# Attention scores by pairs of heads on the two row halves of the TensorE array

## The chip, the cores and the metric

The kernel runs on one core of a Trainium2 chip. The metric is the device time of one execution in microseconds (us): the median of three runs was 967.11 us (966.23 to 969.17). One further execution was taken by the hardware profiler; all rows below are from it. The engines are PE (TensorE matmul), PEld (its weight loads), DVE (VectorE), ACT (ScalarE), POOL (GpSimd) and SP (SyncE, which issues the DMAs).

## The reference, cut to what matters

Attention over 4 batches, 8 heads, 576 positions and 64 channels per head, with a causal window of 128 positions, followed by two feed-forward layers over all 2304 tokens:

```python
scores = (q @ k.T) / sqrt(64)                 # per batch and head
bias   = slope[h] * -abs(i - j)               # slope[h] = 2 ** -(h + 1)
scores = where((i >= j) & (i - j < 128), scores + bias, -1e9)
attn   = exp(scores - max); attn /= attn.sum() + 1e-9
x = (attn @ v), heads side by side            # 2304 x 512
x = ((silu(x @ w_gate) * (x @ w_val)) @ w_out)    # 512 -> 1536 -> 512
y = (g(x @ w_in)) @ w_out2                    # 512 -> 2048 -> 512, g(h) = h * tanh(softplus(h))
```

Everything is float32, and the kernel keeps that precision: either with float32 matmuls, or with operands split into a rounded float32r part ("hi") and the rest ("lo"), of which several rounded matmuls are added up in PSUM.

## The kernel before, in words

**Chunks.** The tokens are cut into five chunks of 512, 384, 512, 512 and 384 (`A_CHUNKS`). A chunk is cut into blocks of up to 128 queries; where a chunk begins or ends inside a batch, a block has 64. A block with `qn` queries needs the keys of its own block and of the one before it (`kn`), so its scores are `qn` rows by `kn + qn` (128 to 256) columns of PSUM. `chunk_plan` packs a chunk's blocks into two PSUM banks of 512 columns (`p.sb`): two blocks of 256 columns and one each of 256 and 128 in chunks 0 and 2; 256+192 and 192+128 in chunk 1; 256+256 and 192+192+128 in chunk 3; 256+256 and 256 in chunk 4.

**Scores of a head.** q and k lie transposed, channels on the partitions. In the first six pairs of heads (`S_FULL`: four of chunk 0, two of chunk 1; "native") the two heads of a pair lie on partitions 0 to 63 and 64 to 127 of one float32 tile, and each head's scores are float32 matmuls over its 64 rows; the profile records two matmuls for each. In the other 14 pairs (28 heads; "split") each head is loaded by itself, twice over, into both halves of `qraw` and `kraw`; `split` makes `Q` (rows 0 to 63 rounded q, rows 64 to 127 the rest of q), `K1` (rounded k in both halves) and `KL` (the rest of k), by two ScalarE and two VectorE instructions (L193, L121, L195, L124). Then two matmuls over all 128 rows, with `K1` and `KL`, give the scores of a block. Native loads alternate between two buffers; `qraw`, `kraw`, `Q`, `K1`, `KL` have one each.

**After the scores.** Per bank VectorE copies the needed half of the window over (`copy_predicated`, L221/L228), and per block adds the bias and takes the maximum (L235); ScalarE takes the exponential with its sum (L239). Per head `norm` inverts the sums (L247, L250) and scales (ScalarE L254, in chunk 0 half on GpSimd, L256). `transp` transposes on PE (L261, into `t_ps`), ScalarE copies out (L267) and GpSimd masks into the two halves of `PT` (L270, L274). `outp` multiplies with v for a pair of heads: its matmuls alternate between column halves of the array, 64 weight columns each (`o_ps`), and the sum is split into hi and lo of `xt`.

**Order.** The first stage is the attention of chunk 0 with the conversion of the first weights beside it. Then come windows: window *ci* holds the gated layer of chunk *ci*, 24 hidden groups (`g_ps`, 12 matmuls of the chunk's columns each) and some 12 out groups (`acc`, 12 matmuls each), and between them the attention pieces of chunk *ci + 1*. The order on PE is written out by hand; the other engines and SP's DMA queue are ordered by the compiler's planner. A piece is S (the scores of one bank), T (a head's transposes) or O (`outp` of a pair), and carries a planned cost (S 1.7 native, 0.87 split; T 0.48; O 0.46 for each key block). After every group, pieces are issued as long as (groups done) x (sum of costs) / (number of groups) exceeds the cost issued so far. The pieces of a step are ordered by `CFG["order"]`: for step `st`, S and S of head `st`, O of the pair finished before, T of head `st - 1` (`st - 2` in chunk 0). With `S` of one head go at its end `norm`, the `split` of the next head and the `load` of the one after that.

**PSUM.** Scores, transposes, O and hidden groups take turns on four banks (`rot`); the four others hold the sums of the out groups.

After the windows come the last gated chunk and the second feed-forward layer (from about 523 us); the change does not touch them.

## Time and profile before

| | us |
|---|---|
| median of three runs | 967.11 |
| profiled execution | 970.98 |
| its span, first to last instruction | 968.9 |
| PE busy | 929.1 (96%) |
| PEld busy | 829.6 (86%) |
| DVE busy | 718.1 (74%) |
| ACT busy | 526.9 (54%) |
| POOL busy | 218.8 (23%) |

The span is what the profile shows; the execution takes 2.1 us more around it. Busy times of matmuls overlap, since the profile models their ends: how long a matmul holds the engine is read from one start to the next. The stages begin at 6.22 (first scores), 60.10 (window of chunk 0), 186.48 (chunk 1), 283.46 (chunk 2), 403.50 (chunk 3) and 522.52 us (last gated chunk).

### The profile page before, as it was taken

How to read it: one execution, taken by the hardware profiler on the slowest of the kernel's cores; microseconds unless marked ns; L12 is line 12 of the kernel's file. 1: busy time of each engine (PE TensorE's matmuls, PEld its weight loads, DVE VectorE, ACT ScalarE, POOL GpSimd, SP SyncE). 2: the span in 40 equal slices, each digit the busy share in tenths (PEclk: the TensorE clock that was granted, in tenths of full speed). 3: DMA queues.
4: the chain of work that ended last, by engine and by line, in shares of the span. 5: the costliest groups of instructions: out<-in, count | busy, mean ns of one | idle time of the engine just before them, and what ended most of it. 6: DMA issues, size and time to landing. Idle time of an engine off the chain costs nothing. (4 is left out here: it accounts for less than half of the span.)

```text
span 968.9 us, 14644 instructions
## 1 busy us (share of the span) xinstructions
PE 929.1 (96%) x5040; PEld 829.6 (86%) x5040; DVE 718.1 (74%) x1359; ACT 526.9 (54%) x1135; POOL 218.8 (23%) x348
## 2 busy tenths in 40 slices
PE   7789999999999999999998998899999999999998
PEld 5447777898998888887877998889999999999997
DVE  5999999788768865478534768778886788777673
ACT  6856667666666664455433445455544645454442
POOL 2531234211110322001014233552012320122000
PEclk9889999999999999999999999999999999999999
DMA  8763334476546743176306993624784257830385
GB/s 285 261 252 143 119 133 148 139 236 220 170 130 195 249 130 115 31 243 216 118 1 221 387 329 106 232 83 145 256 298 148 66 173 251 312 114 21 96 264 183
DMA packets 76921, 174.86 MB, mean 180 GB/s; under 512 B 9136, under 2 KB 52528, under 8 KB 67120
## 3 DMA queue, kind: packets, MB, share of 16 engines
q1 hardware_dynamic: 76848, 173.94, 54.1%
q8 instruction: 40, 0.66, 0.3%
q14 instruction: 33, 0.27, 0.1%
HBM read 138.25 MB, written 35.65 MB: 179 GB/s over the span
## 5 line engine op out<-in xcount | busy, mean ns | idle before, releaser
L114 PE MATMUL g_ps<-xt,w 128*128 128x512 f32 (+1 forms) x1440 | 316.3, 373 | 1.2 <-DVE xt L124 1.2
L114 PEld LDWEIGHTS g_ps<-xt,w 128*128 128x128 f32 x1440 | 258.1, 188 | 37.7 <-issue 2.0
L114 PE MATMUL bk<-xs,win 128*128 128x384 f32 x1008 | 179.0, 336 | 8.1 <-DVE G L684 6.0
L114 PEld LDWEIGHTS bk<-xs,win 128*128 128x128 f32 x1008 | 174.4, 188 | 12.2 <-DVE G L684 9.7
L114 PE MATMUL bk<-op,wout 128*128 128x384 f32 x1008 | 175.8, 334 | 0.8 <-DMA wout<-w2o 0.7
L114 PEld LDWEIGHTS bk<-op,wout 128*128 128x128 f32 x1008 | 174.8, 188 | 1.4 <-issue 1.4
L114 PE MATMUL acc<-hh,ring 128*128 128x512 f32 (+1 forms) x480 | 148.9, 373 | 1.6 <-DVE ring L124 1.5
L121 ACT ACTIVATE op<-G 128x768 fp32r<-128x768 f32 x84 | 70.7, 846 | 66.0 <-PE bk L114 63.4
L114 PEld LDWEIGHTS acc<-hh,ring 128*128 128x128 f32 x480 | 89.0, 188 | 14.9 <-DVE ring L124 2.3
L124 DVE TENSOR_TENSOR op<-G,op 128x768 fp32r<-128x768 f32 x84 | 80.2, 962 | 27.2 <-ACT op L121 26.7
L270 POOL TENSOR_SCALAR_AFFINE_SELECT PT<-PT 128x256 f32<-128x256 f32 (+4 forms) x80 | 42.6, 546 | 253.4 <-ACT PT L267 253.2
L780 POOL TENSOR_TENSOR t<-w 128x256 f32<-128x256 f32 x48 | 44.4, 945 | 224.3 <-DVE win L124 207.7
L114 PE MATMUL acc<-hl,ring 128*128 128x512 f32 (+1 forms) x240 | 88.5, 369 | 1.7 <-DVE hl L124 1.7
L239 ACT ACTIVATE Pt<-Pt,sm 128x128 f32<-128x128 f32 (+1 forms) x160 | 62.5, 392 | 21.5 <-DVE sm L235 21.2
L619 DVE SCALAR_TENSOR_TENSOR t<-t,g_ps 128x512 f32<-128x512 f32 (+1 forms) x60 | 37.6, 627 | 37.4 <-ACT t L618 37.2
L684 DVE TENSOR_TENSOR G<-u,bk 128x384 f32<-128x384 f32 x72 | 38.9, 552 | 31.3 <-PE bk L114 29.2
L1028 ACT ACTIVATE G<-G 128x384 f32<-128x384 f32 x72 | 36.9, 520 | 44.2 <-DVE G L684 44.2
L618 ACT ACTIVATE t<-g_ps 128x512 f32<-128x512 f32 (+1 forms) x60 | 32.8, 547 | 50.3 <-PE g_ps L114 50.2
L627 DVE SCALAR_TENSOR_TENSOR t<-t,g_ps 128x512 f32<-128x512 f32 (+1 forms) x60 | 37.8, 631 | 27.1 <-PE g_ps L114 26.4
L121 ACT ACTIVATE hh<-t 128x512 fp32r<-128x512 f32 (+1 forms) x60 | 35.0, 583 | 41.4 <-DVE t L627 41.4
L254 ACT ACTIVATE Pt<-Pt,sm 128x128 f32<-128x128 f32 (+1 forms) x144 | 46.3, 390 | 12.9 <-DVE sm L250 12.8
L274 POOL TENSOR_SCALAR_AFFINE_SELECT PT<-PT 128x256 f32<-128x256 f32 (+4 forms) x80 | 52.9, 678 | 1.6
(79 smaller groups left out, 1282.2 us busy)
## 6 DMA issues: line engine op xcount, KB each, us to landing
wout<-w2o SPq DMA_DIRECT2D x42, 1024.0 KB, 5.6
wraw<-w SPq DMA_DIRECT2D x16, 1024.0 KB, 5.3
w2o<-chl SPq DMA_DIRECT2D x16, 896.0 KB, 8.6
wst<-w SPq DMA_DIRECT2D x12, 1024.0 KB, 7.2
cw<-w1od SPq DMA_DIRECT2D x24, 512.0 KB, 4.0
w<-w2d SPq DMA_DIRECT2D x24, 512.0 KB, 3.4
w2d<-cw SPq DMA_DIRECT2D x16, 512.0 KB, 4.0
wraw<-w1o SPq DMA_DIRECT2D x6, 1024.0 KB, 6.4
```

The source lines that it names most:

```text
L114: nc.tensor.matmul(out=out, lhsT=lhsT, rhs=rhs, start=start, stop=stop, skip_group_check=True)
L121: return nc.scalar.activation(out=out, in_=in_, func=AF.Copy)
L124: return nc.vector.tensor_tensor(out=out, in0=in_, in1=hi.bitcast(F32), op=ALU.subtract)
L239: nc.scalar.activation(out=Pt[:q.qn], in_=Pt[:q.qn], func=AF.Exp, scale=-1.0, bias=sm[:q.qn, i:i + 1], accum_out=sm[:q.qn, 8 + i:9 + i],)
L254: nc.scalar.activation(out=pt, in_=pt, func=AF.Copy, scale=r)
L270: nc.gpsimd.affine_select(out=here, in_=prev, pattern=[[0, m], [1, n]], compare_op=ALU.is_ge, fill=0.0, base=0, channel_multiplier=-1,)
L274: nc.gpsimd.affine_select(out=prev, in_=prev, pattern=[[0, m], [-1, n]], compare_op=ALU.is_gt, fill=0.0, base=0, channel_multiplier=1,)
L619: nc.vector.scalar_tensor_tensor(out=t[:, :n], in0=t[:, :n], scalar=1.0, in1=st["g"][:, :n], op0=ALU.add, op1=ALU.mult)
L627: nc.vector.scalar_tensor_tensor(out=t[:, :n], in0=t[:, :n], scalar=0.5, in1=vps[:, :n], op0=ALU.mult, op1=ALU.mult)
L684: nc.vector.tensor_tensor(out=out, in0=a, in1=b, op=op)
L780: nc.gpsimd.tensor_tensor(out=x[:, o], in0=a, in1=b, op=ALU.subtract)
L1028: nc.scalar.activation(out=out, in_=in_, func=AF.Mish)
```

## The change

The unit of attention is now a pair of heads instead of a head.

- Loads: one tile `q` and one tile `k` per pair, the heads on partitions 0 to 63 and 64 to 127, one DMA each per segment (a chunk has one or two), for native and split pairs alike, with one buffer for each of the two. Where the chunk's last block has 64 queries, a further DMA loads 64 more columns of q.
- `split` of a split pair: `qh`, `kh` (rounded, ScalarE) and `ql`, `kl` (the rest, VectorE) over 128 partitions, once per pair.
- `score` takes two PSUM banks, one for each head, and issues for every block one pass (native: q, k) or three (split: qh kh, ql kh, qh kl); each pass is two matmuls over 64 rows, one for each head. Split passes have 128 weight columns also where the block has 64 queries.
- `norm` runs once per pair. The order of a step is S O S T T, for the scores of pair `st`, O of pair `st - 2` and the transposes of pair `st - 1`.
- The planned cost of S is worked out from its columns (0.64 to 0.72 for two blocks of a split pair, 0.53 to 0.75 for a native one) and is paid once for two heads; T and O keep theirs.

The core of the diff:

```diff
-    order="SSOT", delay0=2, early=[4], pbufs=10, pump_g=2, pump_p=2, lag=4, lastlag=6, evprio=500,
+    order="SOSTT", early=[2], pbufs=20, pump_g=2, pump_p=2, lag=4, lastlag=6, evprio=500,
...
-            elif s_full(h):
-                q = ap.tile([128, p.n], F32, tag=("qraw", "Q")[pr % 2], name="q32")
-                k = ap.tile([128, p.nk], F32, tag=("K1", "KL")[pr % 2], name="k32")
             else:
-                q = ap.tile([128, p.n], F32, tag="qraw", name="qraw")
-                k = ap.tile([128, p.nk], F32, tag="kraw", name="kraw")
+                q = ap.tile([128, nq], F32, tag="q", name="q")
+                k = ap.tile([128, p.nk], F32, tag="k", name="k")
...
+                nc.sync.dma_start(out=q[:, cq], in_=qT[s.b, hs_, :, sq].rearrange("h d s -> (h d) s"))
+                nc.sync.dma_start(out=k[:, ck], in_=kT[s.b, hs_, :, sk].rearrange("h d s -> (h d) s"))
...
+            qh = ap.tile([128, nq], F32R, tag="qh", name="qh")
+            kh = ap.tile([128, p.nk], F32R, tag="kh", name="kh")
+            nc.scalar.activation(out=qh, in_=q, func=AF.Copy, scale=c)
+            hi_act(kh, k)
+            ql = ap.tile([128, nq], F32R, tag="ql", name="ql")
+            kl = ap.tile([128, p.nk], F32R, tag="kl", name="kl")
             nc.vector.scalar_tensor_tensor(
-                out=Q[64:128], in0=q[64:128], scalar=c, in1=Q[64:128].bitcast(F32), op0=ALU.mult, op1=ALU.subtract
+                out=ql, in0=q, scalar=c, in1=qh.bitcast(F32), op0=ALU.mult, op1=ALU.subtract
             )
-            lo_dve(KL, k, K1)
-            qk[h] = (Q, K1, KL)
+            lo_dve(kl, k, kh)
+            qk[pr] = ((qh, kh), (ql, kh), (qh, kl))
...
+            s_ps = [rot("s_ps") for _ in range(2)]
...
-                    mm(o, Q[:, q.c:q.c + q.qn], K1[:, q.ko:q.ko + w], True, False)
-                    mm(o, Q[:, q.c:q.c + q.qn], KL[:, q.ko:q.ko + w], False, True)
+                m = q.qn if len(passes) == 1 else 128
+                for i, (Q, K) in enumerate(passes):
+                    for e in range(2):
+                        r = slice(64 * e, 64 * e + 64)
+                        mm(
+                            s_ps[e][:m, q.so:q.so + w], Q[r, q.c:q.c + m], K[r, q.ko:q.ko + w],
+                            i == 0, i == len(passes) - 1,
+                        )
...
-            return (a.ci, 1.7 if a.s_full(h) else 0.87, f)
+            if r < a.s_native:
+                return (a.ci, sum((q.kn + q.qn) / 600 for q in blocks), f)
+            return (a.ci, sum(3 * max((q.kn + q.qn) / 2400 + 0.013, 0.107) for q in blocks), f)
...
-            bufs = {"P": CFG["pbufs"], "sm": 8, "PT": 3}
+            bufs = {"P": CFG["pbufs"], "sm": 3, "PT": 3}
```

## Rows read from the trace of the kernel before

**Rows 1.** Stage windows: start:end, length, busy us (instructions), clock, DMA share, GB/s.

```profile
6.22:60.10 53.88, 44.15 (x160) 28.25 (x161) 44.69 (x133) 39.26 (x108) 27.98 (x40) 0.84 0.87 306
60.10:186.48 126.38, 122.58 (x614) 94.17 (x613) 119.48 (x266) 83.63 (x214) 33.69 (x57) 1.00 0.43 141
283.46:403.50 120.04, 120.04 (x642) 97.81 (x641) 80.44 (x199) 69.02 (x197) 23.24 (x70) 1.00 0.47 148
```

**Rows 2.** Waits of PE: us in total, times, longest.

```profile
PE s_ps L114 <- DVE Q L195: 4.0, 3, 1.7
```

**Rows 3.** Timeline of PE, first stage: start, us, instruction, idle before.

```profile
6.22 7.10 PE L114 MATMUL s_ps<-qkv 64*128 64x256 f32 x24 [6.22 <-ACT qkv L185]
...
29.80 1.78 PE L114 MATMUL s_ps<-qkv 64*128 64x256 f32 x8
...
33.57 3.35 PE L114 MATMUL s_ps<-qkv 64*128 64x256 f32 x8
...
42.33 0.66 PE L261 MATMUL t_ps<-cst_sb,Pt 128*128 128x128 f32 x4
...
60.10 2.81 PE L114 MATMUL g_ps<-xt,w 128*128 128x512 f32 x10
```

**Rows 4.** Window of one head's scores in the first stage, columns as above.

```profile
33.57:36.85 3.28, 3.28 (x9) 2.50 (x8) 3.28 (x14) 2.07 (x8) 3.10 (x5) 0.50 1.01 353
```

**Rows 5.** Timeline of PE around two native pieces of chunk 1.

```profile
75.46 1.16 PE L114 MATMUL s_ps<-k,q 64*128 64x256 f32 x4
76.55 0.50 PE L114 MATMUL acc<-hh,ring 128*128 128x512 f32 x1
...
79.50 0.95 PE L114 MATMUL s_ps<-k,q 64*64 64x192 f32 x4
80.38 3.96 PE L114 MATMUL g_ps<-xt,w 128*128 128x512 f32 x16
```

**Rows 6.** Timeline of PE around split pieces of chunks 1 and 4.

```profile
121.19 0.25 PE L114 MATMUL s_ps<-K,Q 128*64 128x192 f32 x1
121.28 0.25 PE L114 MATMUL s_ps<-KL,Q 128*64 128x192 f32 x1
...
418.61 0.28 PE L114 MATMUL s_ps<-K,Q 128*128 128x256 f32 x1
...
419.08 0.40 PE L114 MATMUL acc<-hh,ring 128*128 128x512 f32 x1
...
421.83 0.28 PE L114 MATMUL s_ps<-K,Q 128*128 128x256 f32 x1
```

**Rows 7.** Timeline of PE, a split piece's end and an O piece, chunk 2.

```profile
200.18 0.27 PE L114 MATMUL s_ps<-KL,Q 128*128 128x128 f32 x1
200.29 0.39 PE L114 MATMUL acc<-hh,ring 128*128 128x384 f32 x1
...
202.52 1.74 PE L114 MATMUL o_ps<-PT,v 128*64 128x256 f32 x20
204.19 2.00 PE L114 MATMUL g_ps<-xt,w 128*128 128x384 f32 x10
```

**Rows 8.** Groups by form, split on VectorE: count, busy us, mean ns, idle before.

```profile
L124 DVE TENSOR_TENSOR KL<-kraw,K 128x640 fp32r<-128x640 f32 x16 | 13.1, 820 | 0.6 <-ACT K L121 0.3
L195 DVE SCALAR_TENSOR_TENSOR Q<-qraw,Q 64x512 fp32r<-64x512 f32 x16 | 11.0, 690 | 1.4 <-ACT Q L193 0.9
```

**Rows 9.** Timeline of PE at the last O piece of attention.

```profile
508.15 0.65 PE L114 MATMUL o_ps<-PT,v 128*64 128x256 f32 x2
511.27 2.82 PE L114 MATMUL o_ps<-PT,v 128*64 128x256 f32 x14 [2.47 <-POOL PT L274]
514.02 5.95 PE L114 MATMUL g_ps<-xt,w 128*128 128x512 f32 x24
```

**Rows 10.** Timeline of SP: start, us of issuing, instruction.

```profile
44.23 2.39 SPq L167 DMA_DIRECT2D kraw<-kT  x4
```

**Rows 11.** DMA issues: count, KB each, median us from issue to landing.

```profile
kraw<-kT SPq DMA_DIRECT2D x16, 128.0 KB, 2.9
```

More of the change, by code (lines that the diff above doesn't have):

```diff
@@ L138, in attention, with load @@
         raw, qk, pt_, P_, sums = {}, {}, {}, {}, {}
-        nb_ = len(p.qb)
-        def s_full(h):
-            return h // 2 < s_native
-        def load(h):
-            pr, e = divmod(h, 2)
-            if s_full(h) and e:
-                return
+        nq = p.n + 64 * (p.qb[-1].qn == 64 and not upfront)
+        def load(pr):
             if upfront:
@@ L231, in score @@
-            for q in blocks:
-                Pt = ap.tile([128, 128], F32, tag="P", name="Pt")
-                slope = float(2.0 ** -(h + 1))
-                i = q.idx
-                nc.vector.tensor_tensor_reduce(
-                    out=Pt[:q.qn], in0=s_ps[:q.qn, q.so:q.so + 128], in1=nb[q.kn][:q.qn],
-                    op0=ALU.add, op1=ALU.min, scale=slope, scalar=3.0e38, accum_out=sm[:q.qn, i:i + 1],
-                )
-                nc.scalar.activation(
-                    out=Pt[:q.qn], in_=Pt[:q.qn], func=AF.Exp, scale=-1.0,
-                    bias=sm[:q.qn, i:i + 1], accum_out=sm[:q.qn, 8 + i:9 + i],
-                )
-                P_[h, q.idx] = Pt
@@ new lines, in score @@
+                for i, (Q, K) in enumerate(passes):
[4 more added lines that the diff above has]
+                            i == 0, i == len(passes) - 1,
+                        )
+            twin = [q for q in blocks if q.kn and q.qn == 128]
+            for e in range(2):
+                t = s_ps[e]
+                if len(twin) == 2:
+                    both = t.rearrange("p (u k c) -> p u k c", u=2, k=2)
+                    nc.vector.copy_predicated(
+                        out=both[:, :, 0], mask=own.rearrange("p (u c) -> p u c", u=2), data=both[:, :, 1]
+                    )
+                else:
+                    for q in blocks:
+                        if q.kn:
+                            a = q.so + q.kn
+                            nc.vector.copy_predicated(
+                                out=t[:q.qn, q.so:q.so + q.qn], mask=own[:q.qn, :q.qn], data=t[:q.qn, a:a + q.qn]
+                            )
+                for q in blocks:
+                    h = 2 * pr + e
+                    Pt = ap.tile([128, 128], F32, tag="P", name="Pt")
+                    i = 8 * e + q.idx
+                    nc.vector.tensor_tensor_reduce(
+                        out=Pt[:q.qn], in0=t[:q.qn, q.so:q.so + 128], in1=nb[q.kn][:q.qn],
+                        op0=ALU.add, op1=ALU.min, scale=float(2.0 ** -(h + 1)), scalar=3.0e38,
+                        accum_out=sm[:q.qn, i:i + 1],
+                    )
+                    nc.scalar.activation(
+                        out=Pt[:q.qn], in_=Pt[:q.qn], func=AF.Exp, scale=-1.0,
+                        bias=sm[:q.qn, i:i + 1], accum_out=sm[:q.qn, 16 + i:17 + i],
+                    )
+                    P_[h, q.idx] = Pt
@@ new lines, in norm @@
+        def norm(pr):
+            sm = sums.pop(pr)
+            nc.vector.tensor_scalar(out=sm[:, 16:32], in0=sm[:, 16:32], scalar1=1.0e-9, scalar2=None, op0=ALU.add)
+            nc.vector.reciprocal(out=sm[:, 32:48], in_=sm[:, 16:32])
+            for e in range(2):
+                for q in p.qb:
+                    i = 32 + 8 * e + q.idx
+                    pt, r = P_[2 * pr + e, q.idx][:q.qn], sm[:q.qn, i:i + 1]
+                    if ci or q.idx < 2:
+                        nc.scalar.activation(out=pt, in_=pt, func=AF.Copy, scale=r)
+                    else:
+                        nc.gpsimd.tensor_scalar(out=pt, in0=pt, scalar1=r, scalar2=1.0, op0=ALU.mult, op1=ALU.mult)
@@ L277, in transp @@
                 )
[L278 removed]
+            pt_[h] = pt
         def outp(pr):
```

153 lines of the change are left out of this document (51 added, 102 removed), and 3 rows, old and new, of the table full.

## The prediction, made before the changed kernel ran

> **What bounds the kernel now.** I read the stage windows first, then the waits of TensorE, then its timeline piece by piece. The windows [rows 1] divide the attention work in two. In the first stage (the attention of chunk 0, up to 60.1 us) nothing is full: PE is busy 44.15 of 53.88 us, VectorE 44.69. In the windows of the gated layer (from 60.1 us on) PE is full: 120.04 of 120.04 us in the window of chunk 2, 122.58 of 126.38 in that of chunk 0, where VectorE is nearly full too (119.48). So in the windows every nanosecond of PE issue time in a score, and every wait that PE's fixed order meets, counts one to one; in the first stage the chain from scores over VectorE, ScalarE and GpSimd back to PE counts. The largest wait of PE inside the windows that the change touches is 4.0 us for the split operand Q [rows 2].
>
> **Split scores, streaming.** The pitch is read from start to start, since the busy times of single matmuls overlap. A head now issues two matmuls per query block with all 128 rows. Two blocks of 256 columns take 419.08 - 418.61 = 0.47 us, 0.12 a matmul [rows 6]; one of 128 columns took 200.29 - 200.18 = 0.11, though its columns alone are half of that, so its 128 weight columns set it [rows 7]; one of 192 columns with 64 weight columns took 0.09 [rows 6]. So a block's two matmuls take 0.24, 0.18 and (128 columns, the first of them 0.07) 0.18 us. Per head: chunk 1 0.24 + 3 x 0.18 = 0.78 us, chunk 2 0.90, chunk 3 1.02, chunk 4 0.72; times 4, 8, 8, 8 heads that is 24.2 us, and some 1.2 us more where the weights of the next group are late after a short matmul (0.05 in half of the pieces): 25.4.
> After the change a pair needs three passes, each with the two heads on the two row halves. If the halves run side by side, a pass costs what one matmul costs now: 0.12 for 256 columns, 0.11 for shorter ones (128 weight columns everywhere now). Chunk 1: 3 x (0.12 + 3 x 0.11) = 1.35 us a pair; chunk 2: 3 x (3 x 0.12 + 0.11) = 1.41; chunk 3: 3 x (2 x 0.12 + 3 x 0.11) = 1.71; chunk 4: 9 x 0.12 = 1.08. Times 2, 4, 4, 4 pairs: 19.5 us, 5.9 less.
> Do they run side by side? The nearest row is the O piece, which alternates between column halves: 20 records, eight of 256 and twelve of 128 columns at two passes each, would take 2.99 us one after the other at 2.4 GHz and take 1.67 (204.19 - 202.52) [rows 7]. For row halves there is one hint: the first three heads' scores, laid in turn on the two halves, follow each other without a break and take 7.10 us, while one head took 3.35 at a granted clock of 0.50 [rows 3, 4]. I take side by side; one after the other costs another 19.5 us.
>
> **Split scores, switching.** A 64-row matmul leaves the 128-row form of its neighbours, and at each end of a piece the array changes form. Around the native pieces of chunk 1 this shows: the out group between two of them takes 79.50 - 76.55 = 2.95 us, and between two split pieces 421.83 - 419.08 = 2.75 [rows 5, 6]: 0.20 outside the piece. Inside, the O piece, one form throughout, takes 1.67 us where its columns need 1.49 [rows 7]: 0.18. So 0.4 us for a round trip, with weights that are no longer loaded ahead in it. The change makes 14 pairs x 2 pieces = 28 round trips that weren't there: 11.2 us. The other bound is zero: a float32r matmul with 64 weight columns (128*64) stands among 128*128 ones at a pitch of 0.09 us, with no loss [rows 6], so a form may change for nothing in this type. I take 11.2, since the 64-row native pieces are the nearer row.
> The Trainium skill, TensorEngine Tiling (Array Packing), Key Properties, says that changing the tiling mode drains the engine, while going from tile to tile within a mode does not. The native and O pieces agree with it (0.20 us), the 128*64 rows do not show it; by the rule split scores would cost 11.2 us here, by the 128*64 rows nothing.
> Together: -5.9 + 11.2 = +5.3 us of PE time; by stage about +1.4 in the window of chunk 0, +2.3 in those of chunks 1 and 2, +1.5 in that of chunk 3.
>
> **Native scores of chunk 1.** Four heads pay 76.55 - 75.46 = 1.09 and 80.38 - 79.50 = 0.88 us [rows 5], and 0.20 outside each piece: 2.37 a head, 9.5 in all. Side by side, two pairs pay it: -4.7 us. Not side by side, half of the round trips still goes.
>
> **Waits.** (a) The 4.0 us for Q, three waits [rows 2]. With the planner's costs written out, one group (2.75 us) and a transpose stand between a head's last score and the next head's first in the places that waited; after the change two groups and two transposes at least (6.4 us), while the chain to be hidden keeps its length: scale and round on ScalarE, 0.69 and 0.82 us on VectorE [rows 8]. All 4.0 goes: -2.3 for the two waits in the window of chunk 0, -1.7 for the longest, in that of chunk 3. VectorE also loses 14 pairs of these instructions, up to 1.51 us each, 19 to 21 us in all, and ScalarE about as much, off the path: PE is full beside them.
> (b) The last O piece of attention. A piece is issued once (groups done) x (sum of costs) / 36 exceeds the cost issued so far. In the window of chunk 3 the costs add to 21.64 now; the last transpose stands at 19.32, the last O at 19.80, and both come after group 33: O starts at 508.15, waits 2.47 us for GpSimd's mask, and the next group starts at 514.02 [rows 9], 5.87 us for a piece that needs 1.28 for its columns and the 0.18 from above. With the new costs (sum 13.71, transpose at 11.39, O at 11.87) they come after groups 30 and 32, and two groups, 5.5 us, are more than the 3.1 us from 508.15 to 511.27. -4.4 us.
> (c) A new one. q and k have one buffer now. The load of chunk 1's second native pair must wait until the first pair's last score is done, and the planner leaves one group of 2.75 us between that and the second pair's first score. On SP the load is five DMAs at 2.39 / 4 = 0.6 us, then 2.9 us to landing [rows 10, 11], then the scaling on ScalarE, put at VectorE's 0.69 us for such a tile [rows 8]: 6.6 us, 3.8 late, and a little less where the short last DMA lands sooner. Behind it on SP stand the loads of gate weights, and behind them their conversion on VectorE. Bounds: 0, if PE stands anyway at that early place because VectorE is full, and 6; I take +3. For the third pair three groups (some 9 us) cover load and split: nothing.
> (d) A score piece takes two of the four rotating PSUM banks at once. Two full groups (5.5 us) pass before either is wanted again; the cover is VectorE, nearly full in the window of chunk 0. 0 to +5; I take +1 there.
>
> **First stage.** From the end of the last score (42.33, where the transposes start) to the first hidden group (60.10) pass 17.8 us [rows 3]: the last heads' softmax, GpSimd's scaling and masks, O. Before it, scores and transposes wait in turn. A pair costs PE what a head did, 1.78 us, or 3.35 at the half clock [rows 3], so four head times, 7.1 to 13.4 us, leave PE, but VectorE, with the same score work and the weight conversions, does not shrink: its 53.88 - 44.69 = 9.2 us of idle time are the most that can go [rows 1]. On the other side, scores of two heads, then both transposes, come in larger steps; a head's 3.35 us later at the end is the loss I can see. -9.2 to +3.4, and I take -4: a bit under half of what can go.
>
> **Sum.** First stage -4; window of chunk 0 -4.7 + 1.4 - 2.3 + 3 + 1 = -1.6; chunks 1 and 2 +2.3; chunk 3 +1.5 - 1.7 - 4.4 = -4.6; behind that nothing is touched. Total -7.9 us. The profiled execution took 970.98 us, its span 968.9 and 2.1 around it; 963.1 after. It lay 3.9 above the median of the runs (967.11), so 959.2 for the median. Of this case alone the bounds that I hold likely (first stage -9 to +1, switching 8 to 11.2, new wait 1 to 5) give 952 to 966.
>
> **Rivals** (median times).
> 1. Row halves of rounded passes run one after the other. Against: O's halves overlap, the three first heads too. For: no float32r matmul with 64 rows stands in the trace. 959.2 + 19.5 = 979. Chance 0.09.
> 2. The single buffer decides: slower. The load for pair two waits for PE, blocks SP, and a late weight load holds VectorE and so the hidden groups; pair three's load waits in the same way for pair two. For: VectorE is full in that window, and one group is all the cover. Against: SP's order is planned with these waits in it. Waits of 6, then 4, and a first stage that gains nothing: +3 + 4 + 4 = 970 and up to 974; slower from about 11 us of such waits and losses. Chance 0.14.
> 3. The first stage gives its gain back: weights converted ahead of 60.1 us are then missing, since VectorE is the bound in the window of chunk 0. 959.2 + 4 + 3 = 966: no change. Chance 0.13.
> 4. No cost of switching: 959.2 - 11.2 = 948. Chance 0.08.
> The forecast has 0.56. A measurement of this kernel tells 0.3%, 2.9 us, from no change. Faster: nearly all of the forecast, rival 4, a little of rival 3: 0.65; same 0.18; slower (rivals 1 and 2 in the main) 0.17. The range 949 to 974 leaves out rival 1 and about half of rival 4, with some of the rest: 0.18.
>
> **What would show it.** In the trace after: two s_ps matmuls start a few ns apart and a pass of 256 columns has a pitch of 0.12 us (0.24: rival 1); hidden groups beside a split piece are 0.2 us longer than elsewhere (not: rival 4); no wait for the split operand; O follows its transpose by two groups near 508 us, without the half clock; one wait of some 3 us before the second native pair, released by ScalarE's scaling of q; the first hidden group near 56 us. Wrong as a whole if the first hidden group comes after 60 us, or if waits for q and k add up to over 10.

## The result and the profile after

The changed kernel took 982.18 us (median of 4 runs, 978.67 to 983.49) against 968.05 (4 runs, 966.23 to 969.17) for the kernel before on the same chip: ratio 1.0142, interval 1.0109 to 1.0175. It is slower by 14 us; forecast were 8 us faster. The profiled execution took 983.49 us, its span 981.8. PE is busy 927.2 us instead of 929.1, and VectorE, ScalarE and GpSimd have less to do too:

```profile
PE 927.2 (94%) x5152; PEld 822.9 (84%) x5152; DVE 697.3 (71%) x1291; ACT 511.0 (52%) x1107; POOL 216.4 (22%) x328
```

So the work shrank and the time grew. The windows by stage say where; they answer to [rows 1], and their columns are the same: start:end, length, busy us (instructions) of PE, PEld, DVE, ACT and POOL, then clock, DMA share and GB/s (the last gated chunk begins at 535.51):

```profile
6.14:64.56 58.42, 37.95 (x160) 23.81 (x160) 51.83 (x131) 40.30 (x109) 29.86 (x36) 0.66 0.82 293
64.56:193.72 129.16, 123.24 (x650) 94.50 (x650) 111.56 (x254) 80.91 (x215) 31.83 (x53) 0.98 0.38 126
193.72:299.07 105.35, 99.44 (x647) 92.28 (x646) 69.89 (x175) 59.07 (x159) 12.92 (x20) 0.97 0.47 153
299.07:421.01 121.94, 121.93 (x678) 96.68 (x677) 74.07 (x183) 64.36 (x189) 24.15 (x68) 1.00 0.38 125
421.01:535.51 114.50, 113.33 (x564) 89.36 (x562) 64.64 (x121) 46.51 (x101) 16.82 (x23) 1.00 0.38 127
```

From stage to stage, after less before: first stage +4.5, windows of chunks 0 to 3 +2.8, +8.4, +1.9 and -4.5, the rest -0.1: together +12.9 us, as the spans differ. Read the first row against that of before: PE is busy 6 us less in a stage that is 4.5 us longer, and the granted clock fell from 0.84 to 0.66. In the third row PE, which had been full there but for 2 us, idles 6.

**First stage.** PE's waits in it (us in total, times, longest; the start itself left out):

```profile
PE o_ps L114 <- POOL PT L267: 11.8, 6, 4.1
PE t_ps L254 <- DVE sm L227: 3.3, 2, 3.1
PE t_ps L254 <- ACT cg L405: 1.9, 1, 1.9
```

With the smaller ones they add to 20.5 us, against 9.5 before. What waits, in PE's timeline (start, us, instruction, idle before), answering to [rows 3]:

```profile
15.76 1.09 PE L254 MATMUL t_ps<-cst_sb,Pt 128*128 128x128 f32 x4 [3.10 <-DVE sm L227]
...
39.40 1.77 PE L114 MATMUL s_ps<-qkv 64*128 64x256 f32 x8
42.37 2.05 PE L254 MATMUL t_ps<-cst_sb,Pt 128*128 128x128 f32 x8 [1.20 <-ACT Pt L247]
48.50 1.12 PE L114 MATMUL o_ps<-PT,qkv 128*64 128x256 f32 x2 [4.08 <-POOL PT L267]
...
59.81 1.12 PE L114 MATMUL o_ps<-PT,qkv 128*64 128x256 f32 x2 [3.83 <-POOL PT L267]
...
64.56 3.69 PE L114 MATMUL g_ps<-xt,w 128*128 128x512 f32 x12
```

The last scores are done at 41.2 us, 1.2 earlier than before. But from there to the first hidden group pass 23.4 us, not 17.8. GpSimd's timeline shows the chain between them:

```profile
46.26 1.15 POOL L263 TENSOR_SCALAR_AFFINE_SELECT PT<-PT 128x512 f32<-128x512 f32 x1 [2.83 <-ACT PT L260]
...
48.40 1.69 POOL L263 TENSOR_SCALAR_AFFINE_SELECT PT<-PT 128x512 f32<-128x512 f32 x1
...
50.85 4.53 POOL L249 TENSOR_SCALAR Pt<-Pt,sm 128x128 f32<-128x128 f32 x4
...
56.31 1.88 POOL L263 TENSOR_SCALAR_AFFINE_SELECT PT<-PT 128x512 f32<-128x512 f32 x2 [0.75 <-ACT PT L260]
58.14 3.18 POOL L267 TENSOR_SCALAR_AFFINE_SELECT PT<-PT 128x512 f32<-128x512 f32 x2
```

Masks of pair three, then the four scalings of the last pair in one block, then its four masks, then O at 59.81: every link is that of two heads. The same four masks took 0.63 us each before (the first of them below), beside a VectorE that was idle for part of them; here they take 5.06 us in all beside a full one.

```profile
54.24 0.63 POOL L270 TENSOR_SCALAR_AFFINE_SELECT PT<-PT 128x512 f32<-128x512 f32 x1
```

And while PE waits, its granted clock falls to 0.50, the level of 1.2 GHz (two stretches of the first stage, one of the window of chunk 1; columns as above):

```profile
14.81:28.46 13.65, 9.44 (x33) 5.54 (x34) 12.10 (x34) 11.39 (x31) 7.43 (x12) 0.50 0.98 370
35.29:55.77 20.48, 13.00 (x56) 8.63 (x56) 20.38 (x52) 16.48 (x44) 13.09 (x15) 0.50 0.85 296
...
226.43:229.85 3.42, 3.42 (x13) 3.32 (x12) 3.42 (x6) 1.98 (x5) 2.35 (x2) 0.50 0.66 230
```

With a third stretch (59.18 to 64.56, PE busy 4.29) the clock of 1.2 GHz instead of 2.4 costs about half of PE's busy time there, 13.4 us; before, three shorter ones (PE busy 14.4) cost 7.2. So, as an account of PE's time: waits +11.0, clock +6.2, and the scores that take half as long on PE save the rest: +4.5. The account doesn't make the clock a cause of the length: the first stage of e13 below, whose instructions have the order of the kernel before, spends 29.6 us at the low clock instead of 16.7 and takes 52.3 us instead of 53.9.

**Windows.** PE's waits in the window of chunk 0, then in that of chunk 1:

```profile
PE s_ps L114 <- DVE t L612: 2.0, 1, 2.0
PE o_ps L114 <- DVE sm L227: 1.2, 1, 1.2
PE o_ps L114 <- POOL PT L267: 0.9, 1, 0.9
PE t_ps L254 <- ACT PT L260: 0.8, 1, 0.8
PE s_ps L114 <- ACT q L175: 0.8, 1, 0.8
```
```profile
PE t_ps L254 <- DVE sm L227: 5.9, 3, 2.5
```

No wait for the split operand is left [rows 2]. All but two of these are waits for a PSUM bank that VectorE or ScalarE still reads: a transpose does not use `sm`, it needs the bank whose last reader wrote `sm`. One of the three, in PE's and VectorE's timeline:

```profile
218.18 0.39 PE L114 MATMUL s_ps<-kh,qh 64*128 64x256 f32 x2
...
219.02 4.43 PE L114 MATMUL g_ps<-xt,w 128*128 128x384 f32 x24
...
222.51 0.48 DVE L220 COPY_PREDICATED s_ps<-cst_sb,s_ps 128x128 f32<-128x128 uint8 x2
...
224.91 0.28 DVE L227 CUSTOM_DVE_ANT_0 Pt<-s_ps,cst_sb 128x128 f32<-128x128 f32 x1
...
225.56 0.63 PE L254 MATMUL t_ps<-cst_sb,Pt 128*128 128x128 f32 x4 [2.11 <-DVE sm L227]
```

The pair's last scores take the banks of 218.18; two groups of 384 columns take the other two; 4.4 us later the transpose wants the first again. VectorE gets to it only at 222.51, behind weights whose raw data landed at 220.31, does a part of the next pair's split in between, and lets go at 225.4. In the second of the three cases (253.44) VectorE had waited 3.45 us for ScalarE's step of a conversion; in the third (280.55) it was busy with conversions and the next pair's split.

**What came as forecast.** The row halves run side by side: two matmuls start 3 to 11 ns apart and a pass takes 0.12 us (205.07 - 204.95), where [rows 6] show 0.12 for one matmul of 128 rows:

```profile
204.73 0.39 PE L114 MATMUL s_ps<-kh,qh 64*128 64x256 f32 x2
204.95 0.28 PE L114 MATMUL s_ps<-kh,ql 64*128 64x256 f32 x2
205.07 0.29 PE L114 MATMUL s_ps<-kl,qh 64*128 64x256 f32 x2
```

The first pass of a piece takes 0.22, 0.1 more, the last as much, and the groups beside the piece lose another 0.2 together. The last O now follows its transpose by two groups, without a wait; it answers to [rows 9]:

```profile
517.07 0.49 PE L254 MATMUL t_ps<-cst_sb,Pt 128*128 128x128 f32 x3
517.32 5.75 PE L114 MATMUL g_ps<-xt,w 128*128 128x512 f32 x24
522.99 1.52 PE L114 MATMUL o_ps<-PT,v 128*64 128x256 f32 x16
```

### The profile page after: what moved, and what is told of

Its sections match the earlier page's. It is cut to its first block, busy times and chain, and to the rows that moved or that the text cites. A ratio compares the mean times of both kernels' runs of the same rounds, so it can differ in the third digit from the quotient of the medians.

```text
span 981.8 us, 14458 instructions
## 1 busy us (share of the span) xinstructions
PE 927.2 (94%) x5152; PEld 822.9 (84%) x5152; DVE 697.3 (71%) x1291; ACT 511.0 (52%) x1107; POOL 216.4 (22%) x328
## 4 chain that ended last, share of the span: by engine, by line
PE 72%; DVE 11%; DMA 8%; POOL 3%; ACT 3%; issue 3%; SPq 1%; DVEq 0%; ACTq 0%; POOLq 0%
PE bk L114 31%; PE g_ps L114 24%; PE acc L114 11%; DMA wraw<-w 3%; PE o_ps L114 3%; PE s_ps L114 2%; POOL PT L263 1%; DVE cw L425 1%; DVE G L669 1%; POOL PT L267 1%; PE t_ps L254 1%; DMA w2d<-cw 1%; DVE win L124 1%; DVE cw L431 1%; DMA wout<-w2o 1%
## 5 line engine op out<-in xcount | busy, mean ns | idle before, releaser
L114 PE MATMUL acc<-hh,ring 128*128 128x512 f32 (+1 forms) x480 | 151.7, 379 | 2.8 <-DVE ring L124 2.8
L263 POOL TENSOR_SCALAR_AFFINE_SELECT PT<-PT 128x256 f32<-128x256 f32 (+4 forms) x80 | 49.9, 639 | 323.4 <-ACT PT L260 323.0
L232 ACT ACTIVATE Pt<-Pt,sm 128x128 f32<-128x128 f32 (+1 forms) x160 | 62.4, 392 | 23.4 <-DVE sm L227 23.2
L612 DVE SCALAR_TENSOR_TENSOR t<-t,g_ps 128x512 f32<-128x512 f32 (+1 forms) x60 | 37.7, 628 | 24.6 <-PE g_ps L114 23.9
L124 DVE TENSOR_TENSOR hl<-t,hh 128x512 fp32r<-128x512 f32 (+1 forms) x60 | 40.4, 674 | 20.7 <-ACT hh L121 20.7
L124 DVE TENSOR_TENSOR ring<-cw,ring 128x1024 fp32r<-128x1024 f32 x30 | 38.1, 1270 | 23.3 <-ACT ring L121 23.2
```

The costliest lines, as they stand in the source:

```text
L114: nc.tensor.matmul(out=out, lhsT=lhsT, rhs=rhs, start=start, stop=stop, skip_group_check=True)
L124: return nc.vector.tensor_tensor(out=out, in0=in_, in1=hi.bitcast(F32), op=ALU.subtract)
L232: nc.scalar.activation(out=Pt[:q.qn], in_=Pt[:q.qn], func=AF.Exp, scale=-1.0, bias=sm[:q.qn, i:i + 1], accum_out=sm[:q.qn, 16 + i:17 + i],)
L263: nc.gpsimd.affine_select(out=here, in_=prev, pattern=[[0, m], [1, n]], compare_op=ALU.is_ge, fill=0.0, base=0, channel_multiplier=-1,)
L612: nc.vector.scalar_tensor_tensor(out=t[:, :n], in0=t[:, :n], scalar=0.5, in1=vps[:, :n], op0=ALU.mult, op1=ALU.mult)
```

## Experiments

All lengths in one table (us; the kernel before beside each group of runs had a median of 968.1 to 969.6):

| | median | ratio to before, interval | first stage | window 0 | 1 | 2 | 3 |
|---|---|---|---|---|---|---|---|
| before | 967.11 | | 53.9 | 126.4 | 97.0 | 120.0 | 119.0 |
| after | 982.18 | 1.0142 (1.0109-1.0175) | 58.4 | 129.2 | 105.4 | 121.9 | 114.5 |
| e1 | 978.06 | 1.0108 (1.0080-1.0137) | 56.6 | 129.5 | 100.9 | 121.4 | 114.5 |
| e2 | 985.82 | 1.0175 (1.0142-1.0207) | 58.5 | 132.9 | 100.7 | 121.7 | 114.7 |
| e3 | 980.71 | 1.0126 (1.0109-1.0144) | 55.9 | 128.9 | 99.4 | 124.3 | 117.7 |
| e4 | 989.12 | 1.0221 (1.0184-1.0257) | 66.2 | 132.9 | 100.3 | 122.2 | 114.9 |
| e5 | 980.71 | 1.0123 (1.0090-1.0156) | 56.6 | 130.4 | 101.6 | 121.8 | 114.6 |
| e6 | 980.67 | 1.0122 (1.0089-1.0155) | 57.3 | 131.2 | 100.6 | 122.1 | 114.1 |
| e7 | 982.93 | 1.0142 (1.0110-1.0173) | 57.6 | 131.2 | 100.4 | 122.1 | 114.2 |
| e8 | 1004.5 | 1.0364 (1.0339-1.0388) | 68.3 | 135.2 | 101.9 | 130.0 | 113.0 |
| e9 | 980.32 | 1.0111 (1.0074-1.0148) | 53.7 | 132.3 | 100.1 | 121.7 | 114.8 |
| e10 | 966.53 | 0.9975 (0.9955-0.9995) | 54.2 | 124.9 | 97.2 | 120.0 | 113.5 |
| e11 | 970.86 | 1.0009 (0.9988-1.0030) | 54.5 | 127.0 | 96.9 | 123.6 | 114.3 |
| e12 | 984.69 | 1.0158 (1.0125-1.0192) | 57.9 | 130.7 | 100.9 | 124.6 | 114.8 |
| e13 | 978.68 | 1.0103 (1.0064-1.0142) | 52.3 | 125.1 | 98.3 | 127.9 | 120.8 |
| e14 | 969.05 | 0.9994 (0.9977-1.0010) | 52.8 | 131.4 | 96.8 | 120.0 | 113.4 |
| e15 | 1008.97 | 1.0411 (1.0381-1.0440) | 54.0 | 146.2 | 105.0 | 134.0 | 117.9 |

The kernels e1 to e9, e12 and e15 are edits of the changed kernel, e10, e11, e13 and e14 of the kernel before. Code in the diffs is cut at `...`.

A window's length comes from one profiled execution, and it differs from one execution to the next of the same order of instructions. The traces of e5 and e6 list the same instructions in the same order as that of the changed kernel, on every engine and in SP's queue (by operation, tiles and shapes): their edits moved nothing. In e1 the engines keep that order up to the window of chunk 2. Over these four executions the first stage takes 56.6 to 58.4 us, the window of chunk 0 129.2 to 131.2 and that of chunk 1 100.6 to 105.4. The first stage has this order in e3 and e12 as well: 55.9 to 58.4 over six. In the kernel before, e10 and e13, which share another order there, it takes 52.3 to 54.2. Smaller differences than these are not read as effects below.

**e1, evacuation and normalization first.** On VectorE and ScalarE the instructions behind the scores get a higher priority with the planner.

```diff
+            with tc.high_priority(CFG["evprio"]):
                 for e in range(2):
                     t = s_ps[e]
...
```


> The changed kernel with one edit: the evacuation of the scores (copy of the window half, bias and maximum, exponential) and the normalization of a pair get a high priority in the planner, so VectorE and ScalarE take them ahead of weight conversions and of the next pair's split. Theory A (the banks and the normalization come late because of what stands ahead of them on VectorE): the waits of the transposes for VectorE in the window of chunk 1 (5.9 us in three, with two stretches at the half clock) go and that window falls from 105.4 to 97 to 99 us; the first stage falls from 58.4 to 52 to 55; the whole comes to 966 to 972. Theory B (two heads in one step are too coarse whatever the order): within 3 us of the changed kernel's 982. Theory C (the 64-row passes cost more than was reckoned): no change either.

The order on VectorE and ScalarE came out the same up to the window of chunk 2, so the run doesn't test what it was meant to. It shows something else: the window of chunk 1 is 4.5 us shorter with the same order, and so it is in e4 to e7 and e9 (100.1 to 101.6), where VectorE and ScalarE have that order in this window too. PE is busy 99.44 us there in the changed kernel and 96.4 in each of these six, at a clock of 1.00 instead of 0.97. So 3.0 us of the 8.4 are two stretches at the low clock that only the one execution had, and its waits are 0.7 to 2.2 us longer (5.9 against 3.7 to 5.2); 3 to 4.6 us stay in all of them.

**e2, normalization head by head.** `norm` runs at the end of each head of a pair, over its own half of `sm`.

```diff
+                if g == len(p.sb) - 1:
+                    norm(pr, e)
...
-                    a.norm(r)
```


> The changed kernel with the normalization undone to one per head: each head's sums are inverted and its blocks scaled as soon as that head's last bank is evacuated. Theory B (steps of a pair are too coarse in the first stage, where scaling, transposes and masks of two heads follow each other): the first stage falls from 58.4 by 3 to 5 us, the windows stay, 977 to 979 in all. Theory A: the scaling still stands behind conversions, under 2 us gained; the transposes' waits in the window of chunk 1 stay at 5 to 6 us.

The first stage stays at 58.5: sums taken for two heads at once are not what makes it long.

**e3, the old planned costs.** T and O follow the scores at other distances.

```diff
-            return (a.ci, sum(3 * max((q.kn + q.qn) / 2400 + 0.013, 0.107) for q in blocks), f)
+            return (a.ci, 3.4 if r < a.s_native else 1.74, f)
```


> The changed kernel with the planned costs of a score piece undone to those of two heads before (3.4 native, 1.74 split), so that more groups stand between a pair's last scores and the transposes that reuse their first bank. If the short distance between the two is what makes PE wait in the window of chunk 1: the three waits (5.9 us) and the half-clock stretches go, that window falls by 6 to 8 us; but the last transpose and the last O come close again, and the window of chunk 3 rises by 3 to 4.5 us; 977 to 980 in all. If the distance does not matter: chunk 1's window stays at 105, and the whole rises to 985.

The waits of the window of chunk 1 fall to 2.7 us (3.7 to 5.9 in the seven runs named under e1), and it takes 99.4 us, 1 to 2 less than in e1, e5 and e6, with two banks at once all the same. That fits a share of the distance, but the order on VectorE and ScalarE changed with it. The last window gives 3.2 back, but not for the reason expected. Its last O does move closer to its transpose, by one group, yet doesn't wait; PE waits 2.6 us for a bank that ScalarE still reads (at 469.8) and then has 3.4 us at the low clock.

**e4, banks of their own in the first stage.** The scores of chunk 0 use the four banks of the out groups.

```diff
...
+                s_ps = [
+                    ps.tile([128, 512], F32, tag=f"acc{2 * (g % 2) + e}", name="s_ps", bufs=1) for e in range(2)
+                ]
```


> The changed kernel with the scores of chunk 0 in the four PSUM banks of the out groups, which are empty in the first stage; transposes and O keep the four rotating ones. If the first stage is late because two banks are taken at once: its waits for banks (3.1 us before the first transpose, some 2 us before later scores and transposes) go, and it falls from 58.4 to 53 to 55 us, 977 to 979 in all. If it is late because of the order on VectorE or the pair-wide chain over GpSimd: under 2 us.

The stage gets longer (66.2), with waits of 6.6 us for ScalarE's scaling at 45.0 and 7.1 for GpSimd at 60.3. Banks are not what holds the first stage.

**e5 and e6, conversions of weights later or earlier.**

```diff
-    conv_a=0.1, conv_b=0.9,
+    conv_a=0.4, conv_b=1.2,     # e5
+    conv_a=-0.1, conv_b=0.75,   # e6
```


> The first weights' conversions are spread later over the first stage (issued fully only behind 120% of its pieces instead of 90%, so about a third of the steps before the last scores instead of three quarters, and a quarter of them moves into the window of chunk 0). Theory C (VectorE and ScalarE are held by conversions while the evacuations and the normalization of the last pairs wait): first stage 58.4 -> 53 to 55, window of chunk 0 +2 to +4 since VectorE is 112 of 129 there; whole 978 to 981. Theory T (the tail of the last pair, four scalings and four masks on GpSimd one behind the other, sets the end): first stage within 1 of 58.4, window of chunk 0 longer: 983 to 986.

> The opposite: conversions are issued as early against the scores as in the kernel before (94% of the steps before the last scores, 95% there). Theory C, as far as the tail is concerned: after the last scores VectorE and ScalarE are free, exp and normalization come 3 to 5 us sooner, first stage 54 to 56, whole 978 to 981. If instead conversions anywhere in the stage hold the evacuations, the scores themselves come later by as much as the tail is shorter: first stage 58 to 60. Theory T: masks on GpSimd take 0.63 instead of 1.25 us once VectorE is idle, a gain of 2 to 3 only: first stage 55.5 to 56.5.

As said under the table, the order of the instructions is that of the changed kernel in both, so neither run moves a conversion and neither tests a theory: they are the changed kernel twice more. Their medians lie inside its range of 978.67 to 983.49. Their windows of chunk 1 (columns as above):

```profile
194.04:295.66 101.62, 96.41 (x647) 89.38 (x646) 69.74 (x175) 59.14 (x159) 13.41 (x20) 1.00 0.48 158
194.65:295.21 100.56, 96.41 (x648) 89.39 (x647) 69.75 (x175) 59.15 (x159) 13.41 (x20) 1.00 0.48 160
```

Theory C stays open. In the first stage VectorE is busy 51.83 of 58.42 us (44.69 of 53.88 before), and between the last scores' evacuation, done at 43.70, and the reciprocals of their sums at 49.52 it does conversions for all but 0.6 us.

**e7, all scaling on ScalarE.**

```diff
-                    if ci or q.idx < 2:
-                        nc.scalar.activation(out=pt, in_=pt, func=AF.Copy, scale=r)
-                    else:
-                        nc.gpsimd.tensor_scalar(out=pt, in0=pt, scalar1=r, scalar2=1.0, op0=ALU.mult, op1=ALU.mult)
+                    nc.scalar.activation(out=pt, in_=pt, func=AF.Copy, scale=r)
```


> In chunk 0 all blocks of P are scaled by ScalarE, none by GpSimd (16 instructions moved). Theory T: the four scalings of the last pair (4.53 us on GpSimd) leave the chain and ScalarE does them in some 0.3 us each: first stage 58.4 -> 54 to 55.5, whole 979 to 980. Theory C: ScalarE was behind two conversions there too, so the normalization stays late and at most 1 to 2 us are gained: first stage 56.5 to 58.

GpSimd's 4.5 us leave the chain, and the stage stays within the spread (57.6): the last O then waits 6.3 us for GpSimd's masks, at 59.7. That link alone doesn't set the stage.

**e8, transposes apart.**

```diff
-    order="SOSTT",
+    order="STOST",
```


> Order of a step S T O S T instead of S O S T T: the transposes of a pair are a piece apart, and one of them stands ahead of the last scores. Theory D (transposes right behind a pair's last scores take the banks that its evacuation still holds): the three waits of transposes in the window of chunk 1 (5.9 us) and the two half-clock stretches (2.1) go, window of chunk 1 105.4 -> 97 to 99, and the bank wait at the start of the window of chunk 0 (2.0) goes too; first stage 55 to 58; whole 968 to 975. If the waits are VectorE's being late and not the order of the pieces, other tiles wait in place of t_ps and the window of chunk 1 stays above 103.

Missed by 30 us, and the window of chunk 1 (101.9) came out in neither range. Here two pieces stand between a pair's last scores and its first transpose, five in the changed kernel, and in the first stage PE waits up to 10.6 us at a time for ScalarE's scaling. So the way from scores to scaled P is longer than the two pieces by that much; the order of the changed kernel had hidden most of it.

**e9, chunk 0 head by head, as before.**

```diff
...
+        for st in range(H + 3):
+            if st < H:
+                out += [s_head(st, g) for g in range(2)]
+            if st >= 4 and st % 2 == 0:
+                out.append(o_piece(st // 2 - 2))
+            if 2 <= st < H + 2:
+                out.append(t_piece((st - 2) // 2, st % 2))
...
```


> The changed kernel with chunk 0 alone put back to one head at a time (scores, normalization and the order of the pieces as in the kernel before); chunks 1 to 4 stay in pairs. Theory L (the first stage is set by each pair's way through VectorE, ScalarE and GpSimd: scores that take half as long on PE leave PE waiting, and two heads at once come out of that way later): first stage back to 53.5 to 55, whole 975 to 978.5. Rival (the stage is longer for something else that came with the change: order of loads, sums of a pair, masks): stays above 57, whole 980 to 984.

First stage and window of chunk 0:

```profile
6.25:59.95 53.70, 44.12 (x160) 29.44 (x160) 48.13 (x135) 39.50 (x108) 25.81 (x36) 0.83 0.87 318
59.95:192.24 132.29, 125.32 (x650) 95.91 (x650) 114.37 (x258) 81.97 (x216) 32.86 (x53) 0.97 0.37 123
```

Length, PE time and clock are those of [rows 1] again: pairs are what lengthened the first stage. Which part of the grouping counts the run doesn't tell, since scores, normalization and order go back together. The whole gains less than the stage (1.9 us between the medians): the window behind it, still in pairs, takes 1 to 3 us more, and there PE waits 6.9 us, 5.3 of them for banks that VectorE still reads.

**e10, the last O later, in the kernel before.**

```diff
-            return (a.ci, 0.48, lambda: a.transp(h))
+            return (a.ci, 2.48 if k == n - 1 else 0.48, lambda: a.transp(h))
```


> The kernel before with one planned cost changed (2.48 instead of 0.48 for the very last transpose), so that the last O follows its transpose by four groups instead of none. If the -4.5 of the window of chunk 3 comes from that distance alone, and not from scores by pairs: window of chunk 3 119.0 -> 114.3 to 115, rest within 1, whole 964 to 966 (ratio 0.995 to 0.997). If it comes from elsewhere: 968 to 970.

```profile
497.73 0.49 PE L261 MATMUL t_ps<-cst_sb,Pt 128*128 128x128 f32 x3
...
509.12 1.52 PE L114 MATMUL o_ps<-PT,v 128*64 128x256 f32 x16
```

The window of chunk 3 shrinks by 5.5 to 113.5 us without any scores by pairs. So the planned costs alone can give the -4.5 of the change. This one line is faster than both kernels, by 0.25% (0.05 to 0.45) against the kernel before, a little less than forecast.

**e11, as e10, with two buffers for Q and K1.**

```diff
-            bufs = {"P": CFG["pbufs"], "sm": 8, "PT": 3}
+            bufs = {"P": CFG["pbufs"], "sm": 8, "PT": 3, "Q": 2, "K1": 2}
```


> As e10, and two buffers each for Q and K1 (KL keeps one). If the waits of split scores for Q (4.0 us in all, three of them) come from the single buffer, they go, and VectorE has KL ready in time: another -3 to -4, whole 960 to 962. If they come from VectorE's being late with other work, the wait stays or is released by KL instead: 964 to 966.

```profile
PE g_ps L114 <- DVE sm L235: 4.1, 3, 2.2
PE g_ps L114 <- ACT PT L267: 3.0, 2, 2.6
```

The waits for Q are gone (none is left in the view), and waits of hidden groups for banks, 7.1 us, stand in their place: against e10 the windows of chunks 0 and 2 are 2.1 and 3.6 us longer, and the whole 4.

**e12, one head's passes after the other's.**

```diff
-                for i, (Q, K) in enumerate(passes):
-                    for e in range(2):
+                for e in range(2):
+                    for i, (Q, K) in enumerate(passes):
```


> The changed kernel with the matmuls of a block ordered head by head (three passes of one head, then three of the other) instead of alternating. If alternating is what lets the two row halves run side by side, a pass of 256 columns takes 0.21 to 0.24 us for each head instead of 0.11 to 0.12 for both, split scores +17 to +20, native ones of chunk 1 +3 to +4, first stage +1 to +5: 1003 to 1011. If the hardware overlaps neighbours in whatever order within its queue: below 990.

```profile
205.90 0.29 PE L114 MATMUL s_ps<-kh,ql 64*128 64x256 f32 x2
206.02 0.30 PE L114 MATMUL s_ps<-kl,qh 64*128 64x256 f32 x2
```

The second branch came true (984.69 us, below 990): three matmuls of one row half stand ahead of three of the other in the order of the program, and still the halves run side by side, starting 10 to 18 ns apart, with passes of 0.12 us. Alternating is not needed for that.

**e13, two banks at once in the kernel before.** Both banks of a head's scores are issued with no group between them; nothing else changes.

```diff
+                if heads[st][0].ci:
+                    (ci, cost, f0), (_, _, f1) = todo["S"]
+                    todo["S"] = [(ci, 2 * cost, lambda f0=f0, f1=f1: (f0(), f1()))]
```


> The kernel before with one thing changed: in chunks 1 to 4 the two banks of a head's scores are issued together, with no group between them. Cause D (two banks at once use up the four): waits of PE for banks appear in the windows (9.7 us of waits in all in the kernel before), +4 to +8 with the clock, whole 973 to 978. Cause V (VectorE's order alone): waits within 2 of before, whole 968 to 972.

One of the places, in the window of chunk 2 (PE's timeline):

```profile
358.77 0.28 PE L114 MATMUL s_ps<-KL,Q 128*128 128x128 f32 x1
...
362.48 4.61 PE L114 MATMUL g_ps<-xt,w 128*128 128x512 f32 x12 [3.44 <-ACT PT L267]
```

10 us slower, 1.0103 (1.0064 to 1.0142), some seven tenths of what the change lost, without pairs. In the windows 11 us of waits for banks appear (5.9 of hidden groups for ScalarE's copy of the transposes, the rest for VectorE), the 4.0 for Q go; the window of chunk 2 takes 7.9 us more, that of chunk 0 1.3 less and that of chunk 1 1.3 more. This is cause D, but at other places: in the changed kernel the windows of chunks 0 and 1 got longer. So the run shows what two banks at once can cost in this kernel, and not that they did so there.

**e14, as e10, with native pairs together.** The two heads of a native pair of chunk 1 go out one behind the other.

```diff
...
+                    if h % 2 == 0:
+                        todo["S"] = []
+                    else:
+                        todo["S"] = [
+                            (x[0], x[1], lambda x=x, y=y: (x[2](), y[2]())) for x, y in zip(held, mine)
+                        ]
...
```


> As e10 (last O later), and in chunk 1 the two heads of a native pair are issued together, one behind the other, so that the row halves run side by side as they did in e12; split heads as before; 18 buffers for P instead of 10. Streaming of native scores in the window of chunk 0 7.6 -> 4.2. Cause D: bank waits give 2 to 3 of the 3.4 back, window 123.5 to 125.5 against 124.9 in e10, whole 965 to 967. Cause V: window 121 to 122, whole 962 to 964.

```profile
63.44 2.25 PE L114 MATMUL s_ps<-k,q 64*128 64x256 f32 x8
```

Here the halves did not run side by side: 2.25 us is twice one head's 1.09 [rows 5]. So neither theory is tested. The run shows a price without the gain: the window of chunk 0 takes 131.4 us instead of 124.9 in e10, with 3.3 us more of waits (2.4 of its 5.9 are for banks, 1.9 for ScalarE's scaling) and 5.0 us at the low clock instead of 0.6.

**e15, one bank at a time in the changed kernel.**

```diff
-    order="SOSTT",
+    order="SSOSTST",
...
-                todo["S"] = [s_piece(st, g) for g in range(pairs[st][0].ns)]
+                todo["S"] = [s_head(2 * st + e, g) for e in range(2) for g in range(pairs[st][0].ns)]
...
```


> The changed kernel with scores by head and by bank in every chunk: a piece is one bank of one head, mostly with a group between two of them, so that no two heads run side by side. Cause D: the waits in the windows of chunks 0 and 1 (5.9 and 5.9) fall to 1 to 3 each; split scores take 42 to 47 us instead of 24.6 without the halves side by side, native ones of chunk 1 7.6 instead of 4.2, twice as many switches +5 to +9, first stage 53 to 55: whole 995 to 1008. Cause V: the same prices, but the waits stay at 5 or more in each of the two windows: 1001 to 1014.

Window of chunk 1 (columns as above), and a pass in it:

```profile
206.40:311.35 104.95, 104.95 (x651) 95.95 (x649) 72.08 (x186) 60.50 (x162) 13.10 (x20) 1.00 0.47 153
```
```profile
208.80 0.28 PE L114 MATMUL s_ps<-kh,ql 64*128 64x256 f32 x1
208.92 0.28 PE L114 MATMUL s_ps<-kl,qh 64*128 64x256 f32 x1
```

PE is full again: of 5.9 us of waits none is left, in the window where the changed kernel had them. The price is the other half of the array: one head alone takes the 0.12 us a pass that two took together. Split scores of this window hold PE 14.8 us instead of 7.3 (start to start, summed). In the window of chunk 0 the forecast of cause D failed: PE waits 7.5 us there, 6.3 of them for the operands `q`, `qh` and `ql` and only 1.1 for a bank, and is at the low clock for 17 us. The whole, 1008.97, lies just above D's range and inside V's. Nor are the banks the only difference: each piece has a planned cost of 0.87, normalization goes by head, and a PE that is busy longer gives VectorE more time.

## Why the prediction was wrong

The sum missed the span by 20.8 us (-7.9 against +12.9), and the sign that it named for being wrong as a whole came: the first hidden group at 64.56, after 60. Two steps failed, the first stage and (d). Term by term:

- **First stage, "I take -4": +4.5, outside its bounds (-9.2 to +3.4)**, and +2.0 to +4.5 over the six executions of this order. The step that failed took half of VectorE's idle time as what PE's shorter scores set free. The stage was not held by PE's share of the work: with scores that take half as long, PE waited 11 us more. e9 shows that the pairs are the cause, by going back to single heads (53.7). How they do it is argued from the timelines: the way of each unit from its scores over four engines back to PE gets longer when the unit is two heads, with two heads' evacuations ahead of the exponentials, four scalings, four masks in a row. e2, e4 and e7 each relieve one link and leave the stage at 57.6 us or more, so none of the three alone sets it. Conversions that stand ahead of the pair's evacuations and sums on VectorE are a rival that no run tests. I had named the larger steps, but priced them at one head's 3.35 us of PE time; it is the other engines' time that counted.
- **(d) two banks at once, "0 to +5; I take +1": about +13 in the profiled execution, 10 to 11 in e1, e5 and e6.** In the windows of chunks 0 and 1 PE waits 10.2 us for banks (8.5 to 9.4 in the other three), where 1.5 us were before, and loses some 5 us (3 to 4) at the low clock behind them. The step said that two full groups pass before a bank is wanted again, and that only the window of chunk 0, with VectorE nearly full, is at risk. Two groups of chunk 1 are 4.4 us, not 5.5, and VectorE, 66% busy there, was late for another reason: its order is fixed beforehand, and it stood behind a weight still on its way from memory, behind a step of ScalarE or behind the next pair's split. That PE waits for banks there is read from the trace. How much of it is due to taking two at once is in part argued: e13 (the two banks alone in the kernel before) costs 10 us, but in the window of chunk 2; e3 suggests that the shorter distance between a pair's scores and its transposes, which comes from the new planned costs, has a share; e15 has no wait left in the window of chunk 1, but changes more than the banks.
  The Trainium skill, TensorEngine Tiling (Array Packing), Gotcha 1: PSUM Pressure, says that row tiling raises the pressure on PSUM, since row tiles write to different banks. The bank waits of the changed kernel agree with it (10.2 us, 1.5 before); e13 puts a number on two banks at once alone, without a new row-tiled piece: 10 us. The prediction had weighed another rule of that page and not this one.
- **Split scores, streaming and switching, +5.3: right.** Start to start, they hold PE 24.6 us (25.4 before), where 19.5 of streaming and half of the switching, 5.6, gave 25.1; hidden and out groups of the windows of chunks 1 to 3 take the other half, some 5 us. Rival 4 is out, and rival 1 with it.
- **Native chunk 1, -4.7: right in kind.** 4.7 us instead of 7.6 inside the pieces (start to start, waits left out).
- **(a) waits for Q, -4.0, and (b) the last O, -4.4: right as named.** The window of chunk 3 came out at -4.5 for -4.6. But e11 shows that in the kernel before (a) alone is worth nothing: without these waits it is 4 us slower than e10, by other waits. (b) holds by itself (e10), since behind it follow only groups without attention.
- **(c) the single buffer, +3: 0.75 us**, the wait of 0.8 for ScalarE's scaling of q. Rival 2 forecast slower, for this reason, and the reason was not it.
- **Rival 3** had the first stage give its gain back to the window of chunk 0. There was no gain in the changed kernel; e9, which has the gain, does lose 1 to 3 us in that window.
- **The likely bounds** were added up wrongly at one end: their terms give 949 to 966, not 952. It changes nothing here.

What stays open: why the window of chunk 0 is so much longer in pairs. It took 129 to 135 us with pairs and 131.4 in e14, but 125 to 127 in e10, e11 and, with two banks of one head at once, e13. The waits there are for banks; that two heads' evacuations have to pass VectorE before they are free, where VectorE is nearly full, is argued and not shown.

## What to carry to other kernels

Before halving an engine's work, ask what its slowness was hiding and whether the stage waits for that engine at all: in the first stage here PE only waited 11 us more. Count resources per unit of work as well as time: a unit twice as large takes twice the banks at once and passes every engine of its chain in about twice the time, and a stage bound by such a chain can get longer by it. Where other engines' orders are planned by a compiler, a wait that an edit removes is gained only if what follows has slack, so try the cheap placement alone first (one planned cost, -0.25%), before the rebuild that contains it. And before reading an edit's effect out of one window, see from the two traces whether the order of the instructions changed at all, and profile the unedited kernel more than once: here one window differed by 4.8 us between executions of one and the same order.

## What the hardware showed that I had not expected

- Matmuls on the two row halves run side by side also when three of one half precede three of the other in the program (e12). Four float32 records of one half ahead of four of the other did not (e14). Where the border lies, by count, type or the waits between them, no run here tells.
- One head's split pass on 64 rows takes as long as two heads' side by side, 0.12 us for 256 columns (e15), and as long as a 128-row matmul [rows 6].
- A wait inside a full window can cost more than its length. In the window of chunk 1 the waits of 2.1 and 2.5 us (225.56, 253.44) were each followed by 3.4 us at 1.2 GHz, and PE is busy 3.0 us longer there than in e1, e5 and e6 (99.4 against 96.4), where the waits at the same tiles (1.9 us at most) were not followed by a fall of the clock. Three more executions give no threshold.
